# A tuned attention, MoE and GLU kernel: the two input products of the GLU in a 2x2 form with seven block products in place of eight

## The chip, the cores and the metric

The kernel runs on one core of a Trainium2 chip. The metric is the device time of one execution in microseconds (us). Three runs of the kernel before took 731.0, 731.95 and 732.31 us; the median is 731.95 us.

## The reference, cut to what matters

Three layers follow one another: a gated linear attention, a mixture of experts that sends each token to one expert, and a gated linear unit (GLU). The change touches the GLU and the end of the experts' stage.

```python
def _moe2_ref(x, w1, w2, w3, w_out):      # x: 3072 x 384, w1 and w2: 384 x 1024
    a = x @ w1
    b = x @ w2
    h = a * b @ w3                        # w3: 1024 x 1024
    return (h @ w_out).astype(np.float32) # w_out: 1024 x 384
```

In the kernel `w1` and `w2` are called g1 and g2. The product `w3 @ w_out` is made once, early in the program, and is kept as `wp` (1024 x 384), so the GLU needs g1, g2 and `wp` alone.

## The kernel before

All of the GLU's matrix products are made in an fp32 form with a high and a low part: `split(src, hi, lo, eng)` has ScalarE cast `src` to `hi`, and then `eng` (VectorE, or GpSimd by default) subtract `lo = src - hi`. Each product then is three TensorE passes, hi with hi, hi with lo and lo with hi (`PASSES`).

The experts come first, eight of them, one after the other, each with its window of tokens (376 columns for the last one, expert 7). For each of eight strips `s` of 128 rows of the hidden dimension, `g1_step(e, s)` is nine matmuls; ScalarE then takes the ReLU as the high part of `h`, and VectorE makes the low part of `h`. `g2_step(e, s - 1)` is nine matmuls that read `h` of the strip before; its first matmul needs the high part, its second the low part. While an expert runs, the weights of what comes next are loaded into two "stg" tiles by the queue of SyncE and split in pieces between the steps: `prefetch(ph)` issues the loads and `wsplit.pull(n)` takes up to n pieces. A phase `ph` is half an expert's weights; phases 16 and 17 (`2 * E` and `2 * E + 1`) are the two halves of g1 and g2, each as a load from `gd[0]` and one from `gd[1]`. Phase 15, the second half of expert 7's own weights, is split while the first half of expert 7 runs. In step 2 of expert 7, `x_split(0)` splits the first 512 tokens of the GLU's input `xd`.

The GLU then runs over six blocks `n` of 512 tokens. `xd` holds its input transposed, as three blocks of 128 rows (`kk`, the inner dimension of 384) by the tokens. For each strip `s`, `ab_step(n, s)` makes 9 matmuls of 512 columns into `pa` (g1) and 9 into `pb` (g2); ScalarE copies `pa` out, VectorE multiplies by `pb`, and a split gives the pair `ab`. `out_step` multiplies the pair of an earlier strip with `wp`: 12 matmuls of 384 columns into four accumulators `ob`, which after eight strips are copied out by VectorE and scattered by an indirect DMA that GpSimd issues (`store`).

TensorE, ScalarE, VectorE and GpSimd each take their instructions in the order in which the program lists them. A tile framework adds the waits between them; nothing reorders the queues.

## Time and profile before

| | us |
|---|---|
| median of three runs | 731.95 |
| the profiled execution: its own time | 734.51 |
| the profiled execution: its span, from the first to the last instruction | 732.70 |
| expert 7, from its first matmul to the GLU's first | 398.37 to 423.33 |
| the GLU's matmuls | 423.33 to 725.3 |
| what follows the last matmul | 7.4 |

The profile is one execution. Its times count from the first instruction. What it says of one engine is that engine's busy time and what ended its idle time; a share of busy time is a mean over all stages.

### The profile page before, as it was taken

How to read it: one execution, taken by the hardware profiler on the slowest of the kernel's cores; microseconds unless marked ns; L12 is line 12 of the kernel's file. 1: busy time of each engine (PE TensorE's matmuls, PEld its weight loads, DVE VectorE, ACT ScalarE, POOL GpSimd, SP SyncE). 2: the span in 40 equal slices, each digit the busy share in tenths (PEclk: the TensorE clock that was granted, in tenths of full speed). 3: DMA queues.
4: the chain of work that ended last, by engine and by line, in shares of the span. 5: the costliest groups of instructions: out<-in, count | busy, mean ns of one | idle time of the engine just before them, and what ended most of it. 6: DMA issues, size and time to landing. Idle time of an engine off the chain costs nothing.

```text
span 732.7 us, 13355 instructions
## 1 busy us (share of the span) xinstructions
PE 715.4 (98%) x5170; PEld 656.1 (90%) x5170; DVE 347.7 (47%) x684; ACT 339.2 (46%) x703; POOL 340.1 (46%) x423
## 2 busy tenths in 40 slices
PE   8999999999999999999999999999999999999995
PEld 6999999889999898999999988988888888888885
DVE  8989899977446454455343132222322322323322
ACT  5797878845647566465545532122112122121210
POOL 5466978784877666584564952202202201221002
PEclk9999999999999999999999999999999999999999
DMA  8999999653875878554443330000100100100001
GB/s 162 215 230 230 225 228 236 151 196 95 274 225 183 251 236 247 167 162 140 143 144 93 101 75 1 32 12 1 43 1 1 43 1 1 43 1 23 21 1 46
DMA packets 132030, 85.71 MB, mean 117 GB/s; under 512 B 106481, under 2 KB 114681, under 8 KB 131961
## 3 DMA queue, kind: packets, MB, share of 16 engines
q1 hardware_dynamic: 128489, 74.55, 38.3%
q0 software_dynamic: 3072, 9.46, 3.5%
q8 instruction: 42, 0.69, 0.4%
q10 hardware_dynamic: 400, 0.79, 0.4%
q14 instruction: 27, 0.22, 0.1%
HBM read 70.57 MB, written 14.22 MB: 116 GB/s over the span
## 4 chain that ended last, share of the span: by engine, by line
PE 60%; issue 7%; DMA 4%; POOL 2%; SPq 1%; ACT 1%; DVE 0%; POOLq 0%; ACTq 0%
PE ob L1045 12%; PE pa L1032 11%; PE pb L1032 11%; PE acc L950 11%; PE hb L936 10%; DMA stg<-in_moe_w_dram 3%; PE wpb L185 3%; PE xb L923 1%; DMA gd<-gt 1%; POOL out_dram L1052 1%; POOL gt L230 1%; PE w3b L174 0%; POOL wl L143 0%; ACT wh L142 0%; ACT h L938 0%
## 5 line engine op out<-in xcount | busy, mean ns | idle before, releaser
L143 POOL TENSOR_TENSOR wl<-stg,wh 128x384 fp32r<-128x384 f32 (+1 forms) x119 | 136.2, 1174 | 60.2 <-ACT wh L142 60.1
L1035 DVE TENSOR_TENSOR a<-a,pb 128x512 f32<-128x512 f32 x48 | 33.0, 688 | 181.6 <-PE pb L1032 175.4
L1045 PE MATMUL ob<-wp,ab 128*128 128x384 f32 x576 | 108.2, 339 | 0.0
L950 PE MATMUL acc<-h,wh 128*128 128x448 f32 (+7 forms) x384 | 104.8, 351 | 2.8 <-ACT h L938 1.8
L1045 PEld LDWEIGHTS ob<-wp,ab 128*128 128x128 f32 x576 | 102.3, 188 | 3.8
L936 PE MATMUL hb<-xT,wh 128*128 128x448 f32 (+7 forms) x384 | 102.4, 348 | 0.0
L1032 PE MATMUL pa<-x,wh 128*128 128x512 f32 x288 | 90.2, 394 | 0.0
L1032 PE MATMUL pb<-x,wh 128*128 128x512 f32 x288 | 89.9, 393 | 0.0
L939 DVE SCALAR_TENSOR_TENSOR h<-hb,h 128x448 fp32r<-128x448 f32 (+7 forms) x64 | 37.0, 579 | 107.5 <-ACT h L938 107.3
L1034 ACT COPY a<-pa 128x512 f32<-128x512 f32 x48 | 28.2, 587 | 120.3 <-PE pa L1032 120.3
L1052 POOL DMA_INDIRECT out_dram<-o,didx x24 | 23.2, 968 | 129.3 <-DVE o L1051 126.1
L143 POOL TENSOR_TENSOR x<-xd,x 128x512 fp32r<-128x512 f32 x18 | 22.8, 1296 | 120.5 <-ACT x L142 120.5
L1037 ACT CAST ab<-a 128x512 fp32r<-128x512 f32 x48 | 29.8, 621 | 104.9 <-DVE a L1035 104.9
L950 PEld LDWEIGHTS acc<-h,wh 128*128 128x128 f32 x384 | 70.4, 188 | 7.2 <-ACT h L938 3.2
L142 ACT CAST wh<-stg 128x384 fp32r<-128x384 f32 (+1 forms) x121 | 61.1, 561 | 33.3 <-DMA stg<-in_moe_w_dram 27.3
L936 PEld LDWEIGHTS hb<-xT,wh 128*128 128x128 f32 x384 | 70.8, 188 | 1.2
L936 PE MATMUL hb<-xT,wl 128*128 128x448 f32 (+7 forms) x192 | 66.7, 347 | 0.0
L950 PE MATMUL acc<-h,wl 128*128 128x448 f32 (+7 forms) x192 | 66.6, 347 | 0.0
L1032 PEld LDWEIGHTS pb<-x,wh 128*128 128x128 f32 x288 | 54.2, 188 | 12.7
L1032 PEld LDWEIGHTS pa<-x,wh 128*128 128x128 f32 x288 | 53.6, 188 | 9.2
L938 ACT ACTIVATE h<-hb 128x448 fp32r<-128x448 f32 (+7 forms) x64 | 32.4, 507 | 59.4 <-PE hb L936 59.2
L1032 PE MATMUL pb<-x,wl 128*128 128x512 f32 x144 | 56.9, 395 | 0.0
(202 smaller groups left out, 1281.0 us busy)
## 6 DMA issues: line engine op xcount, KB each, us to landing
stg<-in_moe_w_dram SPq DMA_DIRECT2D x30, 768.0 KB
raw<-in_moe_w_dram SPq DMA_DIRECT2D x28, 512.0 KB
xs<-xsd SPq DMA_DIRECT2D x8, 675.5 KB
q<-in_q_dram SPq DMA_DIRECT2D x24, 192.0 KB
k<-in_k_dram SPq DMA_DIRECT2D x24, 192.0 KB
v<-in_v_dram SPq DMA_DIRECT2D x24, 192.0 KB
f<-in_f_logit_dram SPq DMA_DIRECT2D x23, 192.0 KB
raw<-in_moe_w_out_dram SPq DMA_DIRECT2D x8, 384.0 KB
```

The lines of the kernel that those rows point to most:

```text
L142: A.copy(out=hi, in_=src)
L143: eng.tensor_tensor(out=lo, in0=src, in1=f32(hi), op=ALU.subtract)
L936: PE.matmul(out=b, lhsT=w[x][:, kk, cs], rhs=xT[e][y][:, kk, :], start=(kk + n == 0), stop=(kk == KD - 1 and n == 2))
L938: A.activation(out=h[0], in_=b, func=AF.Relu)
L939: V.scalar_tensor_tensor(out=h[1], in0=b, scalar=0.0, in1=f32(h[0]), op0=ALU.max, op1=ALU.subtract)
L950: PE.matmul(out=acc[d], lhsT=w[x][:, s % 4, d * P:(d + 1) * P], rhs=hs[s][y], start=(s + n == 0), stop=(s == KF - 1 and n == 2))
L1032: PE.matmul(out=b, lhsT=w[x][:, kk, cs], rhs=x2[n][y][:, kk, :], start=(kk + m == 0), stop=(kk == KD - 1 and m == 2))
L1034: A.copy(out=t, in_=pa)
L1035: V.tensor_tensor(out=t, in0=t, in1=pb, op=ALU.mult)
L1037: A.copy(out=ab[s][0], in_=t)
L1045: PE.matmul(out=oacc[t], lhsT=ab[s][x][:, t * P:(t + 1) * P], rhs=wp[:, y, s, :], start=(s + m == 0), stop=(s == KF - 1 and m == 2))
L1052: ins = G.indirect_dma_start(out=out, out_offset=bass.IndirectOffsetOnAxis(ap=didx[:, j:j + 1], axis=0), in_=o, in_offset=None,)
```

## The change

The GLU now takes 1024 tokens at a time, as two blocks of 512, and the strip of g1 and the strip of g2 together as a matrix of two rows. Call the blocks of the weights A11, A12, A13 (g1, for kk = 0, 1, 2) and A21, A22, A23 (g2), and those of the tokens B11, B12 (kk = 0, the two token blocks), B21, B22 and B31, B32. The part over kk = 0 and 1 is a 2x2 product of blocks; it is made with seven block products from the sums S1 = A21 + A22, S2 = S1 - A11, S3 = A11 - A21, S4 = A12 - S2 and T1 = B12 - B11, T2 = B22 - T1, T3 = B22 - B12, T4 = B21 - T2. The part over kk = 2 is plain: four block products. So `group(n, s)` has 11 block products of three passes each, 33 matmuls of 512 columns, where the two token blocks had 36 before. The four outputs (g1 and g2, for both token blocks) lie in four PSUM banks, all that one half of PSUM has; ScalarE, VectorE and GpSimd combine them.

The first token block's `ab` goes to `out_step` in the next group (`then()`); the second's is stored in `later` in plain fp32, over blocks of `xd` that are no longer needed, and split and multiplied with `wp` after the eighth group. `x_sets(n)` makes the nine token operands, `plain_sets` and `mixed_sets` the weights' operands. Of phase 17 the operands are made in the queues behind the groups 0 and 1 of the GLU (`wsplit.pull((6, 9, ...)[s])`), where before `wsplit.drain()` stood ahead of the GLU. Half of phase 15's splits now go to VectorE.

The core of the diff:

```diff
-                split(t[:, i], h[:, i], l[:, i], V if ph == 0 and i % 2 else G)
+                split(t[:, i], h[:, i], l[:, i], V if ph in (0, 2 * E - 1) and i % 2 else G)
...
+    def prefetch_g(ph):
+        hf = ph - 2 * E
+        hl, raw = [], []
+        for i in range(2):
+            hl.append([ring[ph % 2].tile([P, KD, 512], F32R, tag=g, name=g) for g in ("wh", "wl")])
+            raw.append(stage[0].tile([P, KD, 512], F32, tag="stg", name="stg"))
+            SP.dma_start(out=raw[i], in_=phase_src(ph, i, SP))
+            if i == 0:
+                wsplit.add(plain_sets(hl[0], raw[0]))
+                yield
+        sets.append({})
+        wsplit.add(mixed_sets(hf, hl, raw))
...
+    def plain_sets(hl, r):
+        for kk in range(KD):
+            split(r[:, kk], hl[0][:, kk], hl[1][:, kk], V if kk % 2 else G)
+            yield
...
+        one("A23", b, 2, (bh[:, 2], bl[:, 2]), V)
+        yield
+        one("A22", b, 1, (bh[:, 1], bl[:, 1]), G)
+        yield
+        V.tensor_tensor(out=b[:, 2], in0=b[:, 0], in1=b[:, 1], op=ALU.add)
+        V.tensor_tensor(out=b[:, 1], in0=a[:, 0], in1=b[:, 0], op=ALU.subtract)
+        yield
+        V.tensor_tensor(out=b[:, 0], in0=b[:, 2], in1=a[:, 0], op=ALU.subtract)
+        yield
+        one("S1", b, 2, (bh[:, 0], bl[:, 0]), V)
+        yield
+        V.tensor_tensor(out=b[:, 2], in0=a[:, 1], in1=b[:, 0], op=ALU.subtract)
+        ch, cl = third[hf]()
+        yield
+        for i, (n, kk) in enumerate((("S3", 1), ("S2", 0), ("S4", 2))):
+            one(n, b, kk, (ch[:, i], cl[:, i]), V if i == 2 else G)
+            yield
...
-
-        def x_split(n):
-            x2[n] = [m2p[0].tile([P, KD, BT], F32R, name=f"x2{i}", bufs=2) for i in range(2)]
-            src = xd[:, :, n * BT:(n + 1) * BT]
-            for kk in range(KD):
-                split(src[:, kk], x2[n][0][:, kk], x2[n][1][:, kk])
...
+        def open_m2():
+            m2p.append(m2x.enter_context(tc.tile_pool(name="m2", side="right", reuse_waits="tile", bufs=1)))
+            for i, name in enumerate(("B11", "T3", "T2", "T1", "B21", "B31", "T4", "B22", "B32")):
+                xs_of[name] = [m2p[0].tile([P, BT], F32R, name=f"x{i}{p}") for p in "hl"]
+            pairs.append([m2p[0].tile([P, BT], F32R, name=f"ab{p}") for p in "hl"])
...
+        def x_sets(n):
+
+            (b11, b12), (b21, b22), (b31, b32) = [[block(n, kk, t) for t in range(2)] for kk in range(KD)]
+            plus, e1, e2 = (V, G, V) if n else (G, V, V)
...
+            put("B11", b11, e2)
+            yield
+            minus(b11, b12, b11)
+            yield
+            minus(b12, b22, b12)
+            yield
+            put("T3", b12, e2)
+            yield
+            put("T1", b11, e2)
+            yield
+            minus(b11, b22, b11)
+            yield
+            put("T2", b11, e2)
+            yield
+            put("B22", b22, e1)
+            yield
+            put("B21", b21, e1)
+            yield
+            minus(b21, b21, b11)
+            yield
+            put("T4", b21, e2)
+            yield
+            put("B31", b31, e1)
+            yield
+            put("B32", b32, e1)
+            yield
...
+                if e == E - 1:
+                    if s == 0:
+                        bg.drain()
+                        close_w3()
+                        cvx.close()
+                        open_m2()
+                        xs_ids(e)
+                        ahead_x = x_sets(0)
+                    step(ahead_x, 3)
...
-                wsplit.pull((0 if e or s else 2, 3, 2, 2)[s % 4])
+                wsplit.pull((4, 4, 4, 9)[s % 4] if e == E - 1 and s >= KF // 2 else (0 if e or s else 2, 3, 2, 2)[s % 4])
...
-        wsplit.drain()
...
-        def ab_step(n, s):
...
+        def bank2(i, cols, name):
+            return psum[i].tile([P, cols], F32, tag=("ps", "acc")[i], name=name)
+
+        spare = [m1p.tile([P, KD, CAP], F32R, name=f"xT{i}").rearrange("p k w -> p (k w)").bitcast(F32) for i in range(2)]
+        m1t, m5t, m7t, ut = [t[:, i * BT:(i + 1) * BT] for t in spare for i in range(2)]
...
+        def group(n, s, then):
+            w, x = sets[s // 4], xs_of
             cs = slice((s % 4) * P, (s % 4 + 1) * P)
-            for i, b in enumerate((pa, pb)):
-                w = phases[2 * E + s // 4][i]
-                for kk in range(KD):
-                    for m, (x, y) in enumerate(PASSES):
-                        PE.matmul(out=b, lhsT=w[x][:, kk, cs], rhs=x2[n][y][:, kk, :], start=(kk + m == 0), stop=(kk == KD - 1 and m == 2))
-            t = m2p[0].tile([P, BT], F32, name="a", bufs=2)
-            A.copy(out=t, in_=pa)
-            V.tensor_tensor(out=t, in0=t, in1=pb, op=ALU.mult)
-            ab[s] = [m2p[0].tile([P, BT], F32R, name=f"ab{i}", bufs=3) for i in range(2)]
...
-            if 0 in ss:
-                oacc[:] = [bank([P, DM], "ob", tag="acc") for _ in range(NT)]
-            for t, s in [(t, s) for t in ts for s in ss]:
+            ab, bt, bb, at = [bank2(n % 2, BT, name) for name in ("pa", "pb", "pc", "pd")]
+
+            def product(o, a, b, first, last=True):
+                for m, (i, j) in enumerate(PASSES):
+                    PE.matmul(out=o, lhsT=w[a][i][:, cs], rhs=x[b][j], start=(first and m == 0), stop=(last and m == 2), skip_group_check=True)
+
+            def tt(eng, out, a, b, op=ALU.add):
+                eng.tensor_tensor(out=out, in0=a, in1=b, op=op)
+
+            product(ab, "A11", "B11", True)
+            product(bt, "S3", "T3", True)
+            product(bb, "S2", "T2", True)
+            product(at, "S1", "T1", True)
+            A.copy(out=m1t, in_=ab)
+            A.copy(out=m7t, in_=bt)
+            tt(V, ut, m1t, bb)
+            tt(G, m7t, m7t, m1t)
+            A.copy(out=m5t, in_=at)
+            tt(G, m7t, m7t, m5t)
+            product(ab, "A12", "B21", False, False)
+            product(ab, "A13", "B31", False)
+            product(bt, "A22", "T4", False, False)
+            product(bt, "A23", "B31", False)
+            product(at, "S4", "B22", False, False)
+            product(at, "A13", "B32", False)
+            product(bb, "A23", "B32", False)
+            then()
+            tt(V, m1t, ut, bt)
+            tt(V, m1t, m1t, ab, ALU.mult)
+            pair = next_pair()
+            A.copy(out=pair[0], in_=m1t)
+            tt(V, m5t, ut, at)
+            tt(V, pair[1], m1t, f32(pair[0]), ALU.subtract)
+            tt(V, m7t, m7t, bb)
+            later[s] = [m7t] if s == KF - 1 else tails if s == KF - 2 else [block(n, s % KD, s // KD)]
+            for t, c in columns(later[s]):
+                tt(V, t, m5t[:, c], m7t[:, c], ALU.mult)
+            return pair
+
...
-        for n in range(N // BT):
-            lag = 2 if n in (0, N // BT - 1) else 1
...
+        for n in range(NS):
...
+            o1 = [bank2(1 - n % 2, DM, "ob") for _ in range(NT)]
+            last = None
             for s in range(KF):
-                ab_step(n, s)
-                if s == 1:
-                    wsplit.drain()
-                if s == 4 and n + 1 < N // BT:
-                    x_split(n + 1)
-                if s >= lag and (n, s) != (N // BT - 1, KF - 1):
-                    out_step(n, (s - lag,))
-            if n < N // BT - 1:
-                out_step(n, range(KF - lag, KF))
+                pair = group(n, s, lambda: s and out_step(o1, last, s - 1))
+                if n == 0:
+                    wsplit.pull((6, 9, 0, 0, 0, 0, 0, 0)[s])
+                if n == 0 and s == 1:
+                    t = stage[0].tile([P, KD, 512], F32R, tag="stg", name="stg")
+                    pairs.append([t[:, i] for i in range(2)])
+                last = pair
+            o2 = [bank2(n % 2, DM, "ob") for _ in range(NT)]
+            free = list(xs_of.values())
+            second = {0: to_pair(later[0], next_pair())}
+            out_step(o1, last, KF - 1)
+            if end:
+                for s in range(1, KF):
+                    second[s] = to_pair(later[s], free[s], G if s % 2 == 0 else V)
+                    if s == 2:
+                        store(o1, 2 * n * NT)
+                for s in range(KF // 2):
+                    out_step(o2, second[s], s)
+                for t in range(NT):
+                    for s in range(KF // 2, KF):
+                        out_step(o2, second[s], s, (t,))
+                    store(o2, (2 * n + 1) * NT, (t,))
             else:
-                out_step(n, (KF - 3, KF - 2), range(2))
-                out_step(n, (KF - 1,), range(2))
-                out_step(n, range(KF - 3, KF), range(2, NT))
-            store(n)
+                ahead_x = x_sets(n + 1)
+                for s in range(KF):
+                    if s + 1 < KF:
+                        second[s + 1] = to_pair(later[s + 1], next_pair())
+                    out_step(o2, second[s], s)
+                    if s == 0:
+                        store(o1, 2 * n * NT)
+                    step(ahead_x, 2)
+                store(o2, (2 * n + 1) * NT)
```

In expert 7, VectorE's queue had only the low parts of `h` (line 939, for strips 1 to 5 here):

```order
L939 SCALAR_TENSOR_TENSOR h_5920<-hb,h_5919 128x376
L939 SCALAR_TENSOR_TENSOR h_5952<-hb,h_5951 128x376
L939 SCALAR_TENSOR_TENSOR h_6002<-hb,h_6001 128x376
L939 SCALAR_TENSOR_TENSOR h_6033<-hb,h_6032 128x376
L939 SCALAR_TENSOR_TENSOR h_6060<-hb,h_6059 128x376
```

Now the same strips (line 995) stand behind splits of token operands (`x1` is T3, `x3` T1, `x2` T2, `x7` B22, `x4` B21) and of weights (`wl`):

```order
L143 TENSOR_TENSOR x1l<-xd,x1h 128x512
L143 TENSOR_TENSOR x3l<-xd,x3h 128x512
L143 TENSOR_TENSOR wl<-stg,wh 128x512
L995 SCALAR_TENSOR_TENSOR h_5996<-hb,h_5995 128x376
L143 TENSOR_TENSOR x2l<-xd,x2h 128x512
L143 TENSOR_TENSOR x7l<-xd,x7h 128x512
L143 TENSOR_TENSOR x4l<-xd,x4h 128x512
L143 TENSOR_TENSOR wl<-stg,wh 128x384
L995 SCALAR_TENSOR_TENSOR h_6029<-hb,h_6028 128x376
```

Between the low parts of strips 1 and 2 there are now three subtractions, and between those of strips 2 and 3 four, where there was none.

ScalarE's queue for the last three strips of expert 7 was this, ReLU (line 938) and casts of phase 16's and 17's weights (line 142), up to the GLU's first copy (line 1034):

```order
L938 ACTIVATE h_6059<-hb 128x376
L142 CAST wh<-stg 128x512 x3
L938 ACTIVATE h_6088<-hb 128x376
L142 CAST wh<-stg 128x512 x2
L938 ACTIVATE h_6115<-hb 128x376
L142 CAST wh<-stg 128x512 x7
L1034 COPY a<-pa 128x512
```

Now it is this; `ch` are the high parts of S3, S2 and S4, and the `wh` before them that of S1:

```order
L994 ACTIVATE h_6099<-hb 128x376
L142 CAST wh<-stg 128x512 x2
L994 ACTIVATE h_6129<-hb 128x376
L142 CAST wh<-stg 128x512
L142 CAST ch<-stg 128x512 x2
L994 ACTIVATE h_6161<-hb 128x376
L142 CAST ch<-stg 128x512
L1170 COPY xT_6214<-pa 128x512
```

The casts of A23 and A22 now stand ahead of strip 6's ReLU, and those of S1, S3 and S2, which read sums that VectorE makes, ahead of strip 7's.

At the GLU's start VectorE's queue held a product and a split for each strip, and nothing else:

```order
L1035 TENSOR_TENSOR a<-a,pb 128x512
L1038 TENSOR_TENSOR ab_6204<-a,ab_6203 128x512
L1035 TENSOR_TENSOR a<-a,pb 128x512
L1038 TENSOR_TENSOR ab_6231<-a,ab_6230 128x512
```

Now, from the last two instructions of group 0 (line 1164) to the first two of group 1, it holds this (`pc` and `pb` are the banks of the second block's g2 and of the first block's g2; `stg` is the tile of g2's raw weights):

```order
L1164 TENSOR_TENSOR xT_6215<-xT_6215,pc 128x512
L1164 TENSOR_TENSOR xd<-xT_6214,xT_6215 128x512
L143 TENSOR_TENSOR wl<-stg,wh 128x512 x2
L377 TENSOR_TENSOR stg<-stg 128x512
L378 TENSOR_TENSOR stg<-stg 128x512
L1164 TENSOR_TENSOR xT_6215<-xT_6214,pc 128x512
L1164 TENSOR_TENSOR xT_6214<-xT_6215,pb 128x512
```

Four of phase 17's operations stand between the two groups.

## Rows read from the trace of the kernel before

**Rows 1.** The page's parts 1 and 2: busy time by engine, granted clock by slice.

```profile
PE 715.4 (98%) x5170; PEld 656.1 (90%) x5170; DVE 347.7 (47%) x684; ACT 339.2 (46%) x703; POOL 340.1 (46%) x423
...
PEclk9999999999999999999999999999999999999999
```

**Rows 2.** Busy time by stretch: the experts, expert 7, the GLU's matmuls.

```profile
174.80:398.37 223.57, 220.73 (x1234) 213.26 (x1233) 106.84 (x162) 129.41 (x262) 147.97 (x126) 1.00 0.60 186
398.37:423.33 24.96, 24.96 (x145) 24.96 (x145) 5.96 (x12) 11.82 (x24) 19.03 (x16) 1.00 0.42 127
...
423.33:725.30 301.97, 301.89 (x1440) 263.44 (x1439) 80.17 (x122) 68.83 (x117) 50.82 (x66) 1.00 0.06 17
```

**Rows 3.** The chain that ended last: start, us, what.

```profile
398.37 3.12 PE hb L936 x18
...
423.33 2.11 PE pa L1032 x9
...
435.98 2.11 PE ob L1045 x12
...
450.68 2.06 PE pa L1032 x9
```

**Rows 4.** Groups by line and shape: TensorE's matmuls in the GLU.

```profile
L1045 PE MATMUL ob<-wp,ab 128*128 128x384 f32 x576 | 108.2, 339 | 0.0
...
L1032 PE MATMUL pa<-x,wh 128*128 128x512 f32 x288 | 90.2, 394 | 0.0
L1032 PE MATMUL pb<-x,wh 128*128 128x512 f32 x288 | 89.9, 393 | 0.0
...
L1032 PE MATMUL pb<-x,wl 128*128 128x512 f32 x144 | 56.9, 395 | 0.0
L1032 PE MATMUL pa<-x,wl 128*128 128x512 f32 x144 | 56.8, 394 | 0.0
```

**Rows 5.** Groups by line and shape: GpSimd's subtraction, ScalarE's copy and cast, VectorE's operations.

```profile
L143 POOL TENSOR_TENSOR wl<-stg,wh 128x384 fp32r<-128x384 f32 x62 | 62.5, 1037 | 14.2 <-ACT wh L142 14.1
...
L1035 DVE TENSOR_TENSOR a<-a,pb 128x512 f32<-128x512 f32 x48 | 33.0, 688 | 181.6 <-PE pb L1032 175.4 <-ACT a L1034 6.2
...
L1037 ACT CAST ab<-a 128x512 fp32r<-128x512 f32 x48 | 29.8, 621 | 104.9 <-DVE a L1035 104.9
...
L1034 ACT COPY a<-pa 128x512 f32<-128x512 f32 x48 | 28.2, 587 | 120.3 <-PE pa L1032 120.3
...
L1051 DVE COPY o<-ob 128x384 f32<-128x384 f32 x24 | 13.0, 558 | 7.3 <-PE ob L1045 7.3
...
L939 DVE SCALAR_TENSOR_TENSOR h<-hb,h 128x376 fp32r<-128x376 f32 x8 | 4.4, 550 | 17.9 <-ACT h L938 17.9
...
L938 ACT ACTIVATE h<-hb 128x376 fp32r<-128x376 f32 x8 | 3.9, 486 | 11.7 <-PE hb L936 11.7
```

**Rows 6.** Timeline of VectorE and GpSimd around 431.5, and two of VectorE's lines.

```profile
431.52 1.50 DVE L1038 TENSOR_TENSOR ab<-a,ab 128x512 fp32r<-128x512 f32 x1 [0.69 <-ACT ab L1037]
...
428.66 3.80 POOL L143 TENSOR_TENSOR wl<-stg,wh 128x512 fp32r<-128x512 f32 x3 [0.82 <-ACT wh L142]
...
L1038 DVE TENSOR_TENSOR ab<-a,ab x48: 692/693/1499, 431.5 to 720.3; 128x512 fp32r<-128x512 f32 x48
...
L228 DVE SCALAR_TENSOR_TENSOR raw<-raw x20: 692/696/1670, 197.0 to 371.1; 128x512 int32<-128x512 int32 x20
...
L228 DVE SCALAR_TENSOR_TENSOR raw<-raw 128x512 int32<-128x512 int32 x20 | 22.1, 1103 | 0.7
```

**Rows 7.** Timeline of GpSimd and ScalarE in expert 7: a stg tile freed, reloaded, read.

```profile
410.10 3.94 POOL L143 TENSOR_TENSOR wl<-stg,wh 128x384 fp32r<-128x384 f32 x4
...
418.61 1.14 ACT L142 CAST wh<-stg 128x512 fp32r<-128x512 f32 x2 [1.00 <-DMA stg<-gd]
```

**Rows 8.** Timeline of the end: the last copy out and the last store.

```profile
725.26 0.56 DVE L1051 COPY o<-ob 128x384 f32<-128x384 f32 x1 [1.02 <-PE ob L1045]
...
726.20 0.96 POOL L1052 DMA_INDIRECT out_dram<-o,didx  x1 [0.19 <-issue]
```

More of the change, by code (lines that the diff above doesn't have):

```diff
@@ L336, in attn_moe_glu_kernel, with mixed_sets, one @@
     wsplit = Background()
+    sets = []
+    third = []
+    def prefetch_g(ph):
[14 more added lines that the diff above has]
+            yield
+    def mixed_sets(hf, hl, raw):
+        (ah, al), (bh, bl) = hl
+        a, b = raw
+        d = sets[hf]
+        for kk in range(KD):
+            d["A1%d" % (kk + 1)] = ah[:, kk], al[:, kk]
+        def one(n, t, kk, hl, eng):
+            d[n] = hl
+            split(t[:, kk], hl[0], hl[1], eng)
+        one("A23", b, 2, (bh[:, 2], bl[:, 2]), V)
[15 more added lines that the diff above has]
+            yield
     def prefetch(ph):
+        if ph >= 2 * E:
+            yield from prefetch_g(ph)
+            return
         q = A if ph == 1 else SP
@@ L1040, in out_step @@
-        def out_step(n, ss, ts=range(NT)):
-            if 0 in ss:
-                oacc[:] = [bank([P, DM], "ob", tag="acc") for _ in range(NT)]
-            for t, s in [(t, s) for t in ts for s in ss]:
-                for m, (x, y) in enumerate(PASSES):
-                    PE.matmul(out=oacc[t], lhsT=ab[s][x][:, t * P:(t + 1) * P], rhs=wp[:, y, s, :], start=(s + m == 0), stop=(s == KF - 1 and m == 2))
-        def store(n):
-            for t in range(NT):
-                j = n * NT + t
-                o = m2p[0].tile([P, DM], F32, name="o", bufs=NT)
-                V.tensor_copy(out=o, in_=oacc[t])
+        def bank2(i, cols, name):
+            return psum[i].tile([P, cols], F32, tag=("ps", "acc")[i], name=name)
@@ new lines, in attn_moe_glu_kernel, with next_pair, columns @@
+        spare = [m1p.tile([P, KD, CAP], F32R, name=f"xT{i}").rearrange("p k w -> p (k w)").bitcast(F32) for i in range(2)]
+        m1t, m5t, m7t, ut = [t[:, i * BT:(i + 1) * BT] for t in spare for i in range(2)]
+        tails = [t[:, 2 * BT:2 * BT + BT // 2] for t in spare]
+        later = {}
+        used = [-1]
+        def next_pair():
+            used[0] += 1
+            return pairs[used[0] % len(pairs)]
+        def columns(parts):
+            w = BT // len(parts)
+            return [(t, slice(i * w, (i + 1) * w)) for i, t in enumerate(parts)]
@@ new lines, in to_pair @@
+        def to_pair(parts, pair, eng=V):
+            for t, c in columns(parts):
+                split(t, pair[0][:, c], pair[1][:, c], eng)
+            return pair
+        def group(n, s, then):
+            w, x = sets[s // 4], xs_of
+            cs = slice((s % 4) * P, (s % 4 + 1) * P)
+            ab, bt, bb, at = [bank2(n % 2, BT, name) for name in ("pa", "pb", "pc", "pd")]
[32 more added lines that the diff above has]
+                tt(V, t, m5t[:, c], m7t[:, c], ALU.mult)
+            return pair
@@ new lines, in out_step, with store @@
+        def out_step(o, ab, s, ts=range(NT)):
+            for t in ts:
+                for m, (x, y) in enumerate(PASSES):
+                    PE.matmul(out=o[t], lhsT=ab[x][:, t * P:(t + 1) * P], rhs=wp[:, y, s, :], start=(s + m == 0), stop=(s == KF - 1 and m == 2), skip_group_check=True)
+        def store(o, j0, ts=range(NT)):
+            for t in ts:
+                j = j0 + t
+                r = f32(m1p.tile([P, CAP], F32R, name=f"h{j % 2}", bufs=3))[:, 0:DM]
+                V.tensor_copy(out=r, in_=o[t])
@@ L1052, in store @@
                 ins = G.indirect_dma_start(
-                    out=out, out_offset=bass.IndirectOffsetOnAxis(ap=didx[:, j:j + 1], axis=0), in_=o, in_offset=None,
+                    out=out, out_offset=bass.IndirectOffsetOnAxis(ap=didx[:, j:j + 1], axis=0), in_=r, in_offset=None,
                 )
```

32 lines of the change are left out of this document (17 added, 15 removed).

## The prediction

> **What bounds the kernel now.** I read the page first, then the stretches, then the chain that ended last, then the groups by line. TensorE is busy 98% of the span at full granted clock [rows 1], and in the two stretches that the change touches it never rests: 24.96 of 24.96 us in expert 7 and 301.89 of 301.97 in the GLU [rows 2]. The chain there is TensorE's matmuls one behind the other, 1.56 us for nine in expert 7, 2.06 to 2.11 for nine of 512 columns and 2.11 for twelve of 384 in the GLU [rows 3]. So a matmul less in the GLU is time won, and every wait that the change puts in front of TensorE is time lost, from the first one. The other engines have slack as a mean. In expert 7, though, GpSimd works 19.03 of 24.96 us, and VectorE only 5.96 [rows 2].
>
> **What is saved.** Before, the GLU has 864 matmuls of 512 columns (288 + 288 + 144 + 144 [rows 4]). Now it has 24 groups of 33, so 792; 72 go. Nine take 2.06 or 2.11 us [rows 3], a mean of 232 ns each: 72 x 0.232 = 16.7 us. The 576 matmuls of `out_step` stay. The new products run only three matmuls into a bank before they change it; `out_step` does that already and takes 176 ns for 384 columns, 16 above what 384 columns take at 2.4 GHz, and 512 columns in runs of nine are 16 to 21 above theirs. I take no cost for it. If all matmuls ran at the one or the other end (229 or 234 ns), the 792 would be 2.2 us off either way.
>
> **A steady group.** Counted from a group's first matmul, the 11 products (0.69 us each) end at 7.6 and `out_step` of the strip before runs to 9.7. The four first products leave their banks by ScalarE's copies (0.59 each [rows 5]) at 1.4, 2.0 and 3.4, before the products on top of them begin at 2.8, 4.2 and 5.5. At the end VectorE's chain (0.69 an operation) has freed the first two banks 0.7 before the last product ends; the bank of the last product is free 1.4 behind the end, and the next group wants it 3.5 behind the end. So a steady group loses nothing, and `out_step` is the cover: where it is absent (behind group 0 of each pass) the same bank is 0.1 late.
>
> **Expert 7.** Here VectorE and GpSimd are in each other's way. VectorE's subtraction at 431.52 took 1.50 us; it has both inputs in SBUF, and GpSimd was in the last of three subtractions of 1.27 that ended at 432.46; the same line takes 0.69 at the median [rows 6]. So I let a VectorE operation with two SBUF inputs wait until GpSimd's current one is over, after which it needs 0.56, and GpSimd's next one wait for it. The low part of `h` (0.55) reads PSUM and doesn't wait for GpSimd, but it stands behind such operations in its queue. The walk, with the first matmul at 0 (398.37 in the profile): ScalarE's cast of T3 stands ahead of strip 2's ReLU and waits for GpSimd's second difference, done at 6.0; the ReLU comes at 9.16 where its input was there at 6.24. VectorE's low part of strip 2 stands behind a weight split that waits for GpSimd's third difference (8.0 to 9.3); it ends at 10.4, and TensorE wanted it at 9.5: 0.85 lost. Ahead of strip 3's low part stand four subtractions that take turns with three of GpSimd's (1.27, 1.27, 0.97): they end at 11.7, 13.5, 15.0 and 15.6, the low part at 16.15, wanted at 13.5: 2.7 lost. B21 - T2 on GpSimd then ends at 16.9, and ScalarE's cast of T4 waits for it ahead of strip 4's ReLU: 1.5 lost. Strip 5: 0.7. The second raw tile of phase 16 can be loaded only when phase 15's last split has freed its tile, at 20.3; in before the tile freed at 414.04 was there again at 418.61, 4.57 later [rows 7]. So ScalarE stands at A23's cast until 24.8, then come A22 on GpSimd and three sums on VectorE ahead of strip 6's low part: 2.1 lost. S1, S3 and S2 lie ahead of strip 7's in the same way: 2.1. Sum 10.0, and the GLU would start at 35.0 in place of 24.96.
>
> The bounds: the same walk with no turn-taking (0.69 for every subtraction) loses 4.7 us. Taking turns in full loses 10.0: there the 20 subtractions on VectorE wait a mean of 0.51. What the trace shows of such waits is L228, 20 operations beside a GpSimd that is busy 148 of 224 us [rows 2]: mean 1103 ns where 692 is the least, so 0.41 each [rows 6]. That is 20 x 0.10 = 2.0 less. I take 8.0. The Trainium skill (SBUF — State Buffer, Who interferes with whom) states a rule for this: the port pair is locked for a whole instruction, and the later one is fully blocked. By it the full walk's 10.0 would hold; the longest L228 (1670 ns) agrees with it, the mean of the line is what I price by.
>
> **The GLU's start.** Phase 17's operands now stand in the queues behind groups 0 and 1. ScalarE's five casts make group 1's first copy late: 0.5 us. VectorE's chain behind group 1 stands behind A13's, A23's and two sums' work that takes turns with five of GpSimd's operations, so the last product of group 1 waits for VectorE's reading of its bank: 3.2 (nothing without turns). Up to strip 2 there is one tile pair for `ab` in use, so the pair of groups 1 and 2 can be written only when the `out_step` behind the group is over; the last bank is then 0.7 late, twice. Behind group 1, ScalarE's cast of S4 waits for a chain on VectorE (pair, `pc`, product, S2, S1, S4) and stands ahead of group 2's first copy: 3.3 or, with no turns, 2.5. Sum 8.4 with all turns, 4.3 with none. I take 6.7, nearer to the full walk, for the same reason as above.
>
> **The second half of a pass.** Behind the eighth group, `out_step` of the second token block runs 8 x 2.12 us. Each strip's pair is split only when the pair's tile is free, two strips before, and VectorE has between two of these splits two more operations for the next pass, and in the first one four copies out (0.56 [rows 5]). The walk gives 1.0 behind the copies, 0.65 at strip 3, and 0.25, 0.3 and 0.45 where B22, B21 and B31 on GpSimd come into it: 2.65, in two passes 5.3; without the last three 3.3. I take 5.0. The last pass has no next one, and its tiles are free: nothing.
>
> **The end** is as before; only the last store need not wait for GpSimd's issue of the one before (726.20 where the copy ends at 725.82 [rows 8]): -0.3. Expert 6 and all before it keep their order on TensorE and lose nothing.
>
> **The sum**: -16.7 - 0.3 + 8.0 + 6.7 + 5.0 = +2.7 us on the profiled execution's 734.51 (span 732.70 and 1.81 around it), that is 737.2. The median of the runs lies 2.56 below the profiled one, so the forecast is 731.95 + 2.7 = 734.7 us, slower by 0.4%. About 0.2% (1.5 us) is what a measurement of this kernel can tell from no change.
>
> **Rivals.** First, on the faster side: the turns don't bite, since VectorE's and GpSimd's operations meet less than I say. Then the three prices are 4.7, 4.3 and 3.3, and the time is 731.95 - 17.0 + 12.3 = 727.3. For it speaks that VectorE has 19 us free in expert 7; against it that its 20 new subtractions and GpSimd's 13 need the same access, 20 x 0.56 + 11 x 1.27 + 2 x 1.0 = 27 us in a stretch of 25. It decides when the three prices together fall below 17.0 us, which they do if 6.7 of the 11.4 us between the bounds stay away. Second: every turn is taken as in the walk, 10.0 + 8.4 + 5.3 = 23.7, and the time is 731.95 + 6.7 = 738.7. The one pair of rows that shows such a meeting alone speaks for it. By the page of the Trainium skill named above (SBUF — State Buffer, Who interferes with whom) this would be the likeliest case. Third: the products in short runs cost TensorE more than the rows of `out_step` show. If every matmul ran at 234 ns the first forecast would be 736.9; nothing in the trace speaks for more.
>
> **How the numbers follow.** The forecast's own case, 731 to 738, has a chance of 0.45; the faster side 0.33; all turns in full 0.17; the third 0.05. Faster by over 0.2% (below 730.5) gets the faster rival's 0.33; within 0.2% (730.5 to 733.4) 0.15 out of my own case; slower the other 0.52. The range reaches from the faster rival's 727.3 with the matmuls' 2.2 us below it to the full turns with 2.2 above: 725 to 741.
>
> **What would show it.** In the profile of the changed kernel: the GLU has 792 + 576 matmuls, nine of 512 columns still in 2.06 to 2.11 us. Expert 7 takes 30 to 35 us in place of 25, TensorE's waits there end with line 995 on VectorE and 994 on ScalarE, and VectorE's splits of 512 columns have a mean well over 0.69. At the GLU's start groups 1 and 2 wait for lines 1164 and 1170. Between the passes `out_step` waits for line 143 on VectorE. Groups 3 to 7 of each pass show no wait. I am wrong if expert 7 takes under 30 us, or if VectorE's splits stay at 0.7; and wrong the other way if steady groups wait, for then each of 24 pays.

## The result, and the profile after

The changed kernel takes 739.87 us (median of six runs, 738.52 to 742.62), the kernel before 732.10 beside it (six runs, 730.86 to 732.93): 1.0112 times as long, with a 95% interval of 1.0091 to 1.0133. The prediction was slower, 734.7 us, range 725 to 741. The direction and the range hold; the loss is 7.8 us where 2.7 was forecast, and the time lies outside the 731 to 738 of the forecast's own case. The profiled execution took 738.52 us.

The page of the changed kernel, parts 1 and 2 (beside [rows 1]):

```profile
span 736.5 us, 13521 instructions
PE 705.5 (96%) x5098; PEld 644.4 (87%) x5098; DVE 455.4 (62%) x828; ACT 359.8 (49%) x745; POOL 399.8 (54%) x464
PE   8999999999999999999999787999999999999995
PEclk9999999999999999999999998999999999999998
```

TensorE has 9.9 us less work than in [rows 1] and a span that is 3.8 longer. The 23rd to 25th slices, some 405 to 460 us, are no longer full, and in the last of them the granted clock is not either. The stretches there and between the first two passes, as in [rows 2] (expert 7; the GLU's groups 0 to 2; the second half of the first pass; and five pieces of the second one):

```profile
core 0: us, PE busy (x) PEld busy (x) DVE busy (x) ACT busy (x) POOL busy (x), PEclk, DMA share, GB/s
395.11:429.52 34.41, 26.68 (x144) 24.51 (x144) 26.67 (x32) 16.60 (x33) 18.56 (x13) 1.00 0.23 70
429.52:464.28 34.76, 29.30 (x113) 23.19 (x113) 22.95 (x29) 10.80 (x20) 16.01 (x11) 0.90 0.17 46
513.01:536.07 23.06, 22.00 (x121) 20.53 (x120) 17.87 (x29) 9.72 (x19) 11.18 (x13) 1.00 0.10 35
...
447.00:449.00 2.00, 1.71 (x4) 1.42 (x5) 1.83 (x4) 0.00 (x0) 0.00 (x0) 0.59 0.00 0
449.00:451.00 2.00, 2.00 (x8) 2.00 (x8) 0.38 (x1) 0.00 (x0) 0.00 (x0) 0.56 0.00 0
451.00:457.00 6.00, 3.75 (x18) 2.74 (x16) 3.88 (x6) 2.88 (x6) 0.48 (x1) 1.00 0.00 0
457.00:459.00 2.00, 1.44 (x3) 1.17 (x4) 1.87 (x2) 1.49 (x4) 2.00 (x2) 0.65 0.00 0
459.00:461.00 2.00, 2.00 (x6) 1.62 (x5) 0.00 (x0) 0.00 (x0) 1.92 (x3) 0.50 0.00 0
```

Expert 7 takes 34.41 us where it took 24.96. The three groups are 99 matmuls of 0.232 and twelve of 0.176, which is 25.1; they take 34.76. The second half is 120 matmuls of 0.176, which is 21.1; it takes 23.06, and 23.1 again in the second pass. TensorE's waits from expert 7 on (in total, times, longest):

```profile
PE acc L1006 <- DVE h L995: 7.7, 6, 2.1
PE pa L1161 <- ACT xT L1170: 3.2, 2, 2.8
PE pc L1161 <- DVE xT L1164: 2.2, 1, 2.2
PE ob L1199 <- DVE stg L143: 1.1, 4, 0.4
PE ob L1199 <- DVE abl L143: 1.0, 2, 0.5
```

These are lines that the prediction named, and no other; ScalarE's line 994, which it named too, ends none of these waits. In a steady group the chain is TensorE's alone, with nine matmuls of 512 columns in 2.1 us as in [rows 3]:

```profile
485.97 0.70 PE pa L1161 x3
486.66 0.69 PE pb L1161 x3
487.35 0.71 PE pc L1161 x3
...
488.75 1.37 PE pa L1161 x6
```

So the saving is whole, and all of the loss lies at the three places where operands are made. At the GLU's start there is something that the prediction does not have. TensorE there, in order of time, with what it waited for in brackets:

```profile
447.29 0.78 PE L1161 MATMUL pc<-x8h,wh 128*128 128x512 f32 x1 [2.23 <-DVE xT L1164]
457.56 0.80 PE L1161 MATMUL pa<-x4h,wh 128*128 128x512 f32 x1 [2.82 <-ACT xT L1170]
```

Behind the waits of 2.23 and 2.82 us the clock is granted at 0.50 to 0.65 in the pieces from 447 to 451 and from 457 to 461: the lower of its two levels, 1.2 GHz, for most of that time. The shares that are missing in these four pieces, 0.41, 0.44, 0.35 and 0.50 of 2.00 us, are 3.4 us of clock at most.

### The profile page after: what moved, and what is told of

Its sections match the earlier page's. It is cut to its first block, busy times and chain, and to the rows that moved or that the text cites. A ratio compares the mean times of both kernels' runs of the same rounds, so it can differ in the third digit from the quotient of the medians.

```text
span 736.5 us, 13521 instructions
## 1 busy us (share of the span) xinstructions
PE 705.5 (96%) x5098; PEld 644.4 (87%) x5098; DVE 455.4 (62%) x828; ACT 359.8 (49%) x745; POOL 399.8 (54%) x464
## 4 chain that ended last, share of the span: by engine, by line
PE 58%; DVE 7%; DMA 3%; ACT 3%; issue 2%; POOL 2%; SPq 1%; POOLq 0%; DVEq 0%; ACTq 0%
PE acc L1006 11%; PE hb L992 10%; PE ob L1199 10%; PE pa L1161 7%; PE pb L1161 6%; PE pd L1161 6%; PE pc L1161 4%; DMA stg<-in_moe_w_dram 3%; PE wpb L185 3%; DVE wl L143 1%; PE xb L979 1%; ACT wh L142 1%; DVE stg L143 1%; DMA stg<-gd 1%; DVE h L1205 1%
## 5 line engine op out<-in xcount | busy, mean ns | idle before, releaser
L1164 POOL TENSOR_TENSOR xT<-xT,xT 128x512 f32<-128x512 f32 x48 | 62.8, 1308 | 132.9 <-ACT xT L1171 129.5
L1164 DVE TENSOR_TENSOR xT<-xT,pc 128x512 f32<-128x512 f32 x48 | 32.8, 683 | 39.4 <-PE pc L1161 39.2
L1164 DVE TENSOR_TENSOR xT<-xT,pb 128x512 f32<-128x512 f32 x24 | 16.5, 689 | 64.3 <-PE pb L1161 64.2
L1199 PE MATMUL ob<-wp,abh 128*128 128x384 f32 x176 | 46.0, 343 | 0.0
L1199 PE MATMUL ob<-wp,stg 128*128 128x384 f32 x228 | 44.3, 338 | 1.1 <-DVE stg L143 1.1
L516 POOL TENSOR_SCALAR_AFFINE_SELECT am<-am 128x512 f32<-128x512 f32 x48 | 29.4, 637 | 25.7 <-ACT am L515 25.7
L1199 PEld LDWEIGHTS ob<-wp,stg 128*128 128x128 f32 x228 | 39.6, 188 | 3.8 <-DVE stg L143 3.0
L1206 POOL DMA_INDIRECT out_dram<-h,didx x24 | 24.2, 1010 | 27.0 <-DVE h L1205 24.6
L185 PE MATMUL wpb<-wo,w3t 128*128 128x384 f32 x192 | 36.8, 340 | 0.0
L992 PEld LDWEIGHTS hb<-xT,wl 128*128 128x128 f32 x192 | 36.1, 188 | 0.7
```

The source lines that it names most:

```text
L185: PE.matmul(out=o, lhsT=t[:, x, j, :], rhs=wo[:, y, j, :], start=(j + n == 0), stop=(j == KF - 1 and n == 2))
L516: G.affine_select(out=m[:, hb], in_=m[:, hb], pattern=[[0, NP], [1, P]], compare_op=ALU.is_ge, fill=0.0, base=0, channel_multiplier=-1)
L992: PE.matmul(out=b, lhsT=w[x][:, kk, cs], rhs=xT[e][y][:, kk, :], start=(kk + n == 0), stop=(kk == KD - 1 and n == 2))
L1164: eng.tensor_tensor(out=out, in0=a, in1=b, op=op)
L1199: PE.matmul(out=o[t], lhsT=ab[x][:, t * P:(t + 1) * P], rhs=wp[:, y, s, :], start=(s + m == 0), stop=(s == KF - 1 and m == 2), skip_group_ ...
L1206: ins = G.indirect_dma_start(out=out, out_offset=bass.IndirectOffsetOnAxis(ap=didx[:, j:j + 1], axis=0), in_=r, in_offset=None,)
```

## The experiments

**Theory.** In expert 7 VectorE's and GpSimd's subtractions block each other, so the low parts of `h` are late. At the GLU's start phase 17's work stands in the queues ahead of what frees the banks and the pair. In the second half the copies out stand ahead of the splits. **Rivals:** the queues alone are too long, whoever does the work; the single tile pair for `ab` makes the loss at the start. Ratios below are to the kernel before, run beside them on the same chip.

**`lock`: GpSimd is as busy, but reads nothing.**

```diff
     def split(src, hi, lo, eng=G):
         A.copy(out=hi, in_=src)
+        if eng is G and blind[0]:
+            for _ in range(3):
+                G.memset(f32(lo), 0.0)
+            return
...
+                if blind[0]:
+                    for _ in range(3):
+                        plus.memset(out, 0.0)
+                    return
                 plus.tensor_tensor(out=out, in0=x, in1=y, op=ALU.subtract)
...
+                blind[0] = e == E - 1
```

> In expert 7 every GpSimd subtraction (the four token differences, the low parts of weights) is replaced by three memsets of its output, about as long in all, which read nothing; the waits between engines stay. The token differences and those low parts are left out of the result. Theory A (VectorE's subtractions with two SBUF inputs and GpSimd's take turns): VectorE's line-143 subtractions in expert 7 fall from a mean of 1.12 us to 0.70, and expert 7 from 34.3 to about 30 us, the time from 739.9 to about 735.5. Theory B (the order in the queues alone makes the low parts of h late): expert 7 stays at 33 to 35 us.

Measured: 733.25 us in one run, where before had a median of 732.56. The time itself says less than the stretches: of the 5.0 us by which the span is shorter than the change's, 3.3 lie in expert 7, 1.0 ahead of it and some 0.6 behind the last matmul. VectorE and GpSimd in expert 7, in order of time, first the changed kernel:

```profile
403.48 1.65 DVE L143 TENSOR_TENSOR wl<-stg,wh 128x512 fp32r<-128x512 f32 x1 [0.27 <-ACT wh L142]
404.53 4.86 POOL L143 TENSOR_TENSOR wl<-stg,wh 128x512 fp32r<-128x512 f32 x3
405.06 0.54 DVE L995 SCALAR_TENSOR_TENSOR h<-hb,h 128x376 fp32r<-128x376 f32 x1
405.51 1.31 DVE L143 TENSOR_TENSOR x2l<-xd,x2h 128x512 fp32r<-128x512 f32 x1
406.75 1.78 DVE L143 TENSOR_TENSOR x7l<-xd,x7h 128x512 fp32r<-128x512 f32 x1
408.45 1.49 DVE L143 TENSOR_TENSOR x4l<-xd,x4h 128x512 fp32r<-128x512 f32 x1
```

and the same instructions in `lock`:

```profile
403.10 0.69 DVE L149 TENSOR_TENSOR wl<-stg,wh 128x512 fp32r<-128x512 f32 x1 [0.27 <-ACT wh L144]
404.00 0.55 DVE L1001 SCALAR_TENSOR_TENSOR h<-hb,h 128x376 fp32r<-128x376 f32 x1 [0.21 <-ACT h L1000]
404.52 4.65 POOL L147 MEMSET wl<- 128x512 f32 x9
405.26 0.69 DVE L149 TENSOR_TENSOR x2l<-xd,x2h 128x512 fp32r<-128x512 f32 x1 [0.72 <-ACT x2h L144]
405.87 0.69 DVE L149 TENSOR_TENSOR x7l<-xd,x7h 128x512 fp32r<-128x512 f32 x1
406.47 0.69 DVE L149 TENSOR_TENSOR x4l<-xd,x4h 128x512 fp32r<-128x512 f32 x1
```

The stretch of expert 7:

```profile
394.07:425.22 31.15, 26.62 (x146) 24.58 (x144) 17.83 (x31) 16.62 (x33) 19.25 (x39) 1.00 0.26 79
```

GpSimd's column is as long as before (19.25 against 18.56), and at 404.5 it is at work for 4.65 us where it was for 4.86; yet VectorE's subtractions take 0.69 each where they took 1.31 to 1.78, and its column falls from 26.67 to 17.83. So it is not GpSimd's being busy that stretches them, but that it reads SBUF at the same time. The low part of `h`, which reads PSUM, is 0.54 and 0.55. Expert 7 is 3.3 us shorter. The Trainium skill (SBUF — State Buffer, Who interferes with whom) says that a VectorE instruction with two SBUF inputs contends with a GpSimd instruction that reads SBUF, and not with one that only writes it; these rows agree, 1.31 to 1.78 beside subtractions and 0.69 beside memsets.

**`all_v`: expert 7's subtractions on VectorE alone.** The core of the edit:

```diff
-V if ph in (0, 2 * E - 1) and i % 2 else G
+V if ph == 2 * E - 1 or ph == 0 and i % 2 else G
...
-            plus, e1, e2 = (V, G, V) if n else (G, V, V)
+            plus, e1, e2 = (V, G, V) if n else (V, V, V)
...
-        one("A22", b, 1, (bh[:, 1], bl[:, 1]), G)
+        one("A22", b, 1, (bh[:, 1], bl[:, 1]), G if hf else V)
```

> In expert 7 all of GpSimd's 13 subtractions go to VectorE, nothing else changes. Theory A (turns): VectorE gets 13 operations more, but each of its 33 takes 0.69 or less, so that its work is 27 us in place of 27 (20 x 1.12 + 8 x 0.55); the waits of ScalarE for GpSimd's 1.3 us differences get shorter, and expert 7 takes 30 to 33 us in place of 34.3: the time is 736 to 739, ratio to the kernel before 1.005 to 1.010. Theory B (queue order): 13 x 0.65 = 8 us more stand in the queue ahead of the low parts of h, expert 7 takes 38 us or more, the time is 744, ratio 1.016.

Measured: 735.29 us (732.73 to 737.25), ratio 1.0032 (1.0013 to 1.0051). The stretch of expert 7:

```profile
397.30:427.77 30.47, 27.29 (x145) 25.68 (x144) 25.45 (x45) 16.50 (x33) 0.00 (x0) 0.94 0.34 101
```

VectorE does 45 instructions in 25.45 us where it did 32 in 26.67, and expert 7 is 3.9 us shorter. An engine taken out of the work made the stage faster. The time is 0.7 below the 736 to 739 that were expected, and part of it is not expert 7's. The GLU's first three groups, whose code and queues are the change's, take:

```profile
427.77:460.95 33.18, 27.68 (x113) 21.70 (x113) 22.79 (x28) 10.80 (x20) 16.05 (x11) 0.95 0.14 28
```

TensorE's waits there are 5.5 us (5.4 in the change), but the clock is at its lower level only behind the last of them, of 2.83 us, and is granted at 0.95 in place of 0.90. The stretch is 1.6 us shorter for it.

**`spread`: the GLU's start.** Phase 17's pieces go behind groups 0 to 3, and a second tile pair is there from the first group (in tiles of `h`, 384 and 128 columns):

```diff
+        hw = [[m1p.tile([P, CAP], F32R, name=f"h{i}", bufs=3) for _ in range(2)] for i in range(2)]
+        pairs.append([(a[:, 0:3 * P], b[:, 0:P]) for a, b in hw])
...
-                    wsplit.pull((6, 9, 0, 0, 0, 0, 0, 0)[s])
-                if n == 0 and s == 1:
+                    wsplit.pull((3, 4, 4, 1, 0, 0, 0, 0)[s])
+                if n == 0 and s == 3:
```

> Phase 17's operands are made behind the groups 0 to 3 (3, 4, 4 and 1 pieces) in place of 0 and 1 (6 and 9), and a second tile pair for ab is there from the start, in six pieces of the idle h tiles. Theory: the 9.9 us lost between the GLU's first matmul and the end of group 2 (34.9 us in place of 25.0) come from the queues behind groups 0 and 1 and the one pair; about 8 of them go, the granted clock of that stretch goes from 0.90 to 1.00, and the time is about 732, ratio 1.000. Rival: it is the raw tiles' loads or the wait for expert 7's last work, which are as before: nothing changes, 739.9, ratio 1.011.

Measured: 730.47 us (727.47 to 733.26), ratio 0.9973 (0.9956 to 0.9990). The GLU's first three groups:

```profile
430.95:456.30 25.35, 25.35 (x113) 20.91 (x113) 19.74 (x26) 9.04 (x17) 12.87 (x9) 1.00 0.24 62
```

TensorE is busy through all of it at full clock: 25.35 us in place of 34.76. So none of the start's loss is the GLU's own.

**`queue` and `pair2`: the two halves of that edit apart.** `queue` has the pulls of `spread` and one tile pair up to the fourth group; `pair2` has the second pair and the pulls of the change.

> Of the mend at the GLU's start one half alone: phase 17's 15 pieces are spread over groups 0 to 3 in place of groups 0 and 1, and there is one tile pair until the fourth group. Theory A (the queues of VectorE and ScalarE make the loss, 7.0 of the 8.4 us in the prediction's walk): most of the 9.4 us comes back, 731 to 733. Theory B (the one tile pair makes it, and the clock falls after its waits): little comes back, 737 to 739.

> The other half alone: a second tile pair from the first group, with phase 17's work behind groups 0 and 1 as in the change. Theory A (the queues make the loss): 1.4 us comes back, the prediction's price of the one pair, so 738 to 739. Theory B (the one tile pair makes it): most of the 9.4 us comes back, 731 to 733.

Measured: `queue` 732.96 us (731.79 to 736.27), ratio 1.0008 (0.9994 to 1.0023); `pair2` 736.98 (734.63 to 737.47), ratio 1.0050 (1.0033 to 1.0068). Off the change's 739.87 that is 6.9 and 2.9 us, and 9.4 together in `spread`. By the ratios, each to the kernel before beside it, the three are 7.6, 4.5 and 10.2. The queues make most of it, and the one pair at least twice the 1.4 of the walk. The first three groups of `queue`, then of `pair2`:

```profile
433.83:462.29 28.46, 26.88 (x113) 21.42 (x113) 18.91 (x23) 8.72 (x16) 13.19 (x9) 0.96 0.16 38
432.74:463.81 31.07, 28.43 (x113) 22.75 (x113) 22.58 (x28) 11.42 (x22) 16.08 (x11) 0.91 0.15 36
```

TensorE's waits there are 1.6 us in `queue` and 2.6 in `pair2`, where the change has 5.4. The missing share of the clock is 1.1 us of the stretch in `queue` (0.04 of 28.46), 2.8 in `pair2` and 3.4 in the change. So of the 6.3 us that `queue` wins in this stretch 3.8 are waits and up to 2.3 clock; of the 3.7 of `pair2`, 2.8 and up to 0.6. In both executions the clock was already at its lower level when the GLU began.

**`late_store`: the copies out of the first token block go behind the last split of the second half.**

```diff
-                    if s == 0:
+                    if s == 6:
                         store(o1, 2 * n * NT)
```

> The copies out of the first token block's four accumulators (VectorE, 0.5 us each) move from behind the first to behind the seventh out_step of a pass's second half. Theory: the copies make the split for strip 2 late, 1.0 us and some more behind it in each of two passes; 2 to 3 us go, 737 to 738, ratio 1.007 to 1.008. Rival: the chain over GpSimd's splits of B22 and B21 ends the pass anyway: under 1 us, ratio 1.010 to 1.012.

Measured: 748.87 us (747.58 to 751.36), ratio 1.0232 (1.0206 to 1.0259): 9 us slower than the change, a miss for both theories. Its chain of waits at the second pass's first group, its later part in order of time:

```profile
544.19 0.96 POOL out_dram L1206
...
545.45 0.96 POOL out_dram L1206
...
546.52 1.23 POOL xT L1164
...
547.77 0.70 DVE xT L1164
...
548.51 1.51 PE pa L1161 x3
```

Eight scatters now stand together in GpSimd's queue, some 1.27 us from one to the next, ahead of group 0's two sums. VectorE waits for the sum that ends at 547.75, and TensorE for VectorE's reading of the bank that it frees: 4.17 us in the second pass and 4.1 in the third; behind the first of the two the clock is 0.82 over 9.5 us.

**`late_v`: the late store again, and group 0's two sums of the later passes on VectorE.**

```diff
-            tt(G, m7t, m7t, m1t)
+            tt(V if n and s < 1 else G, m7t, m7t, m1t)
...
-            tt(G, m7t, m7t, m5t)
+            tt(V if n and s < 1 else G, m7t, m7t, m5t)
```

> The late store again, with the two sums that GpSimd makes in the first group of the second and the third pass on VectorE. Theory A (the 9 us that the late store lost are GpSimd's: eight scatters of about 1.27 us each stand in its queue ahead of those sums, VectorE waits 7.3 us for them and TensorE 4.2 for VectorE's reading of a bank): the time falls to 737 to 740, at or just under the changed kernel's 739.9. Theory B (the accumulators of the first token block are copied out too late for the next pass whoever makes the sums): it stays above 745.

Measured: 735.28 us (734.30 to 735.46), ratio 1.0047 (1.0029 to 1.0065). The 9 us are GpSimd's queue. The second half of the first pass is:

```profile
514.40:535.80 21.40, 21.11 (x121) 20.79 (x120) 16.62 (x27) 9.83 (x19) 5.40 (x5) 1.00 0.00 1
```

That is 1.66 us less than in the change, 3.3 in two passes; the time is 1.7 below what was expected.

**`both` and `both_act`.** `both` joins `all_v` and `spread`; in `both_act` ScalarE also makes the first block's four copies, at their old place.

> Both mends at once: GpSimd's 13 subtractions of expert 7 on VectorE, and at the GLU's start phase 17's work spread over groups 0 to 3 with a second tile pair from the first group. Theory A (the two losses are separate waits at separate places): the gains add. The changed kernel's 739.9 us less 4.6 (what the first alone gave) less 9.4 (what the second alone gave) is 725.9 us, a ratio of 0.992 to the kernel before. Theory B (part of each gain is the same: the clock that falls after long waits, which either mend keeps up): the time is 728 to 730. In the profile A wants expert 7 at 30 to 31 us and the GLU's first three groups at 25 to 26.

> As the kernel with both mends, and behind the eighth group of the first two passes ScalarE, not VectorE, makes the four copies out of the first token block's accumulators (0.59 us each). Theory A (VectorE's queue is late with the splits of the second half because the copies stand in it; the prediction put 1.0 us a pass on them, and the run with the late store showed the waits at the splits fall from 2.1 to 0.6 us): 1.5 to 2 us less than with both mends alone, about 724. Theory B (ScalarE's casts of the next strips, which now stand behind the copies, are late by as much): the same time as with both mends alone, or 1 us more.

Measured: `both` 724.74 us (723.72 to 725.56), ratio 0.9892 (0.9874 to 0.9910): the two gains add, within 1.2 us. `both_act` 724.15 (723.82 to 725.08), ratio 0.9884 (0.9867 to 0.9902); the difference of the two lies within their intervals. That is 0.6 us less where theory A wanted 1.5 to 2, so theory A missed. The second half takes 22.68 us, 0.4 less. VectorE's split of the pair for strip 2, the first behind the copies, in the change, in `both_act` and in `late_v`:

```profile
521.51 0.68 DVE L143 TENSOR_TENSOR abl<-xd,abh 128x512 fp32r<-128x512 f32 x1
509.48 0.69 DVE L143 TENSOR_TENSOR abl<-xd,abh 128x512 fp32r<-128x512 f32 x1
521.23 0.69 DVE L143 TENSOR_TENSOR abl<-xd,abh 128x512 fp32r<-128x512 f32 x1
```

Counted from the half's first matmul (513.01, 501.39 and 514.40) it begins at 8.50, 8.09 and 6.83 us. In `both_act` ScalarE's casts stand behind the copies, so the split comes only 0.41 earlier; with the copies out of the way it comes 1.67 earlier. The stretches are shorter by the same, 0.38 and 1.66.

Of expert 7's remaining 5.1 us in `both` (396.01 to 426.04) most lies at its end, behind a load; ScalarE there, in order of time:

```profile
417.04 1.14 ACT L142 CAST wh<-stg 128x512 fp32r<-128x512 f32 x2 [2.58 <-DMA stg<-gd]
418.09 0.47 ACT L994 ACTIVATE h<-hb 128x376 fp32r<-128x376 f32 x1
```

**`raw`: that load goes to a tile that is free.** As `both_act`, with:

```diff
-            raw.append(stage[0].tile([P, KD, 512], F32, tag="stg", name="stg"))
+            if hf == 0 and i:
+                raw.append(raw0[0]())
+            else:
+                raw.append(stage[0].tile([P, KD, 512], F32, tag="stg", name="stg"))
...
+        def xs_raw():
+            return m1p.tile([P, 4, XW], F32, name="xs").rearrange("p c w -> p (c w)")[:, 0:KD * 512].rearrange("p (k f) -> p k f", k=KD)
```

> As the kernel with both mends and ScalarE's copies, and the second raw tile of phase 16 goes to a tile that is free throughout expert 7 (that of the token windows), in place of the one that phase 15's last split frees. Theory A (what is left of the loss in expert 7, 5.1 us, is mostly ScalarE standing at A23's cast until that load lands, 2.6 us, with strips 6 and 7 behind it): expert 7 takes 27 to 28 us in place of 30, and the time is 721 to 722 us. Theory B (the number of VectorE's subtractions ahead of the low parts makes what is left, and the load is only the last of several): expert 7 stays at 29.5 or more, and the time at 723.5 to 724.5.

Measured: 722.44 us (721.22 to 723.91), ratio 0.9878 (0.9855 to 0.9901). By the times alone it cannot be told from `both_act`; in the profile the wait at the cast is gone and expert 7 is 28.10 us (395.66 to 423.76). ScalarE again:

```profile
414.00 1.13 ACT L142 CAST wh<-xs 128x512 fp32r<-128x512 f32 x2
416.01 0.49 ACT L998 ACTIVATE h<-hb 128x376 fp32r<-128x376 f32 x1 [0.88 <-PE hb L996]
```

The next ReLU now waits for TensorE, not for the load. It is theory A, just above what it gave (27 to 28 us and 721 to 722).

**`best`: all that gained**, with the late store and `late_v`'s sums in place of ScalarE's copies.

> All that gained, together: expert 7's subtractions on VectorE alone, phase 17 over four groups with the second pair, the early raw tile, and in place of ScalarE's copies the late store with the first group's two sums on VectorE. Theory A (the late store with these sums takes 1.66 us off each of two second halves, where ScalarE's copies take 0.4): 722.4 + 0.8 - 3.3 = 719.9 us, a ratio of 0.984, and both second halves at 21.4 us. Theory B (with the first passes shorter GpSimd's scatters reach further into the next pass and TensorE waits there): 722 or more.

Measured: 720.06 us (718.11 to 722.41), ratio 0.9850 (0.9828 to 0.9872). Expert 7, the first three groups and the second half of the first pass:

```profile
395.02:423.12 28.10, 25.96 (x146) 24.56 (x144) 25.32 (x45) 16.50 (x33) 0.00 (x0) 1.00 0.40 130
423.12:448.47 25.35, 25.35 (x113) 20.89 (x113) 19.57 (x25) 9.02 (x17) 12.87 (x9) 1.00 0.11 14
497.18:518.60 21.42, 21.12 (x122) 20.80 (x120) 16.64 (x27) 9.83 (x19) 5.40 (x5) 1.00 0.00 1
```

Of the 23.1 us that the changed kernel lost at its three places (9.45 + 9.7 + 3.9), 4.0 are left (3.1 + 0.3 + 0.6), and 1.5% of the time is gained on the kernel before with the change's own arithmetic.

## Why the prediction was right, and where its sizes were off

The range holds by 1.1 us, and partly by luck: 739.87 lies beyond the forecast's own case (731 to 738, chance 0.45) and nearest to the second rival's 738.7 (0.17). That rival's three prices add up to 23.7 us and the three places lost 23.1, but not by its mechanism: not every turn was taken, and up to 3.4 us of the loss is lower clock, which no price has.

Counted from expert 7's first matmul to the end of the span, the changed kernel takes 341.39 us (736.5 less 395.11) and the one before 334.33 (732.70 less 398.37): +7.06. What lies ahead of it varies from one execution to the next: that matmul comes at 394.1 to 398.2 us in the traces of the changed kernel and its variants. The steps give the sum:

| step | predicted | measured in the trace |
|---|---|---|
| 72 matmuls | -16.7 | -16.7 |
| expert 7 | +8.0 (4.7 to 10.0) | +9.45 |
| the GLU's start | +6.7 (4.3 to 8.4) | +9.7 |
| second halves | +5.0 (3.3 to 5.3) | +3.9 |
| the end | -0.3 | +0.7 |
| sum | +2.7 | +7.1 |

**The saving and the steady group** are as worked out: 0.69 to 0.71 for three matmuls of 512 columns and no wait in the chain. The short runs cost nothing, so the third rival falls.

**Expert 7**: the mechanism is right, shown by `lock` and `all_v`. In the change ten of VectorE's 20 subtractions with two SBUF inputs took 1.24 to 1.78 us and the others 0.54 to 0.69, and 9.45 us were lost, beside the walk's 10.0. With no two subtractions meeting, `both` loses 5.1 and `lock` 6.2, beside the walk's 4.7. The term was mis-sized by 1.45, and not where I doubted it: the 20 take 22.4 us in the change and 13.5 in `lock`, so each waits a mean of 0.44, nearly the 0.41 that I took from L228 [rows 6]. One step that failed shows in the walk itself: I took all of the 2.0 us of wait by which this falls short of the full walk off the loss, though there only half of the wait reaches TensorE (20 x 0.51 = 10.2 us of it make 10.0 - 4.7 = 5.3). Half of 2.0 would have given 9.0. The other is the walk without turns, 4.7 us, which both runs exceed.

Which of the two weighs more stays open: the turns cost 9.45 - 5.1 = 4.4 us by `both` and 9.45 - 6.2 = 3.3 by `lock`, the 3.3 that I had priced (8.0 - 4.7). Neither run is quite the walk's case: `both` has 13 operations more in VectorE's queue, and three memsets of `lock` hold GpSimd 1.69 us where a difference took 1.29.

The Trainium skill (SBUF — State Buffer, Who interferes with whom) calls the port pair that VectorE and GpSimd share an exclusive lock; that it is held for a whole instruction it says of VectorE's 2-port modes. The rows agree where subtractions meet: the last of the three of VectorE's beside GpSimd's three ends at 409.94, 0.55 after GpSimd's at 409.39. Taken in full, this rule made 10.0 of the term, nearer to the 9.45 than my 8.0.

**The GLU's start** failed most, by 3.0 us and beyond its upper bound (its lower bound adds up to 4.4, not 4.3). The waits are the ones named: of 9.7 us the trace shows 5.4 as TensorE's waits, at lines 1164 and 1170, and up to 3.4 as lower clock. The step that failed is that a wait costs only its own length; every matmul of [rows 3] had full clock, and the walk priced all of them so. The waits alone, 5.4, are less than the 6.7 that I took. What the clock costs shows beside `all_v`: with the same waits and one fall of the clock in place of two, the start takes 1.6 us less, so two falls make some 3.2 to 3.4. The last 0.9 us are in neither, and their cause stays open. No run tells the turns at the start from the order of the queues there, so the walk's 3.2 us for those turns is untested by itself.

**The second halves**: the price was 1.1 us too high. The share of the copies, 1.0 a pass in the walk, was more: without them ahead of the splits (`late_v`) 1.66 of the 1.95 that the first pass lost is gone.

**The end**: the scatter is issued at 729.22, 0.28 behind the end of the copy, where it was 0.38 before, so the -0.3 was -0.1. But 7.3 us pass from there to the end of the span, where before they were 6.5 [rows 8]. In `best` they are 6.3 (710.12 to 716.4), so this is no property of the change.

The faster rival (727.3) needed the turns to stay away. `both` took expert 7's turns away and the start's queues with them, and is at 724.7.

## What to carry to other kernels

Here the trade of matrix work for additions was paid where the additions are made for the first time and at the seams, not in the steady loop. So price the first group, the last one and the seams by walking each engine's queue in order. Two engines that read SBUF for the same stage can be slower than one of them alone, and a free engine's queue is not free if something on the critical path stands behind it there, as the eight scatters show. Where TensorE waits, look at the granted clock behind the wait and count that too.
